# Loads, casts and weight issues of the first two chunks put in a new order, in a windowed-attention and max-out FFN kernel

## The chip, the cores and the metric

The kernel runs on one core of a Trainium2 chip. The metric is the device time of one execution in microseconds (us), lower is better; a kernel's time is the median of its runs.

The core's engines each work through a list of instructions of their own, in the order in which the program names them: TensorE (PE, with its weight loads shown apart as PEld), VectorE (DVE), ScalarE (ACT), GpSimd (POOL) and SyncE (SP). An engine waits on semaphores where an instruction needs another engine's result, and whatever stands behind the waiting instruction on that engine waits too. Transfers from HBM run on 16 DMA engines; here SP issues the loads of Q, K and V and the stores, and POOL issues the loads of the weights, which turn float32 into bf16 on the way.

## The reference

Attention with a window of 128 positions and 4 sink positions, for 4 batches, 8 heads, 768 positions and 64 columns; then a feed-forward layer whose hidden value is the maximum of three products.

```python
scores = scale * np.matmul(q, k.transpose(0, 1, 3, 2))      # 4 x 8 x 768 x 768
keep = is_sink | in_window                                  # pos < 4, or 0 <= i - j < 128
scores = np.where(keep, scores, -1000000000.0)
a = np.exp(scores - np.max(scores, axis=-1, keepdims=True))
a = a / (np.sum(a, axis=-1, keepdims=True) + 1e-09)
attn_out = np.matmul(a, v)
x = attn_out.transpose(0, 2, 1, 3).reshape(3072, 512)
h = np.maximum(np.maximum(x @ w1, x @ w2), x @ w3)          # 512 x 768 each
return (h @ w_out).astype(np.float32)                       # 768 x 512
```

## The kernel before

The 3072 rows are cut into 12 chunks of 256, three to a batch. A chunk holds 128 partitions of two neighbouring rows each. For every chunk the kernel

- loads Q, K and V (`load`, L107), 512 KB each, as float32; with `parts=2` a load is cut into two halves of four heads, `part=0` for heads 0 to 3 and `part=1` for heads 4 to 7. A `gate` writes one element of the target on POOL first, so that the load can't be issued before POOL has come to that place;
- casts Q and K to bf16, in halves of four heads (`cast_qk`, L118), and V in four pieces of 64 partitions (`cast_v`, L123), straight into `vb`, which has a column of ones beside each head;
- transposes Q and K by PE through PSUM (`turn`, L138, copied out at L142 for Q and L149 for K; `turn2`, L164, does the same for a half of K and then of Q in one PSUM bank, copied out at L171 and L168);
- computes scores for a pair of heads (`score`, L331), for which `premask` may first write the mask into PSUM by a matmul with the identity (L311); exponentials on ACT (`expo`, L398); where there was no premask, a multiplication by the mask on DVE (`mask`, L406);
- scores the sink positions (`sink_score`, L423, its exponential at L427) and takes their V rows out by a matmul with a selector (`sink_v`, L437), which DVE copies into `vs` (L440). In the second and third chunk of a batch the output sum begins with them: `av_open` multiplies them (L453) into four PSUM banks, one for each pair of heads, and reads `vs`;
- multiplies by V (`av`, L471) and divides by the sum (`norm`, L481 and L484, on DVE; `then=False` leaves it to a later call);
- transposes the result (`xpose`, L496, copied out at L498) and runs the FFN: `ffn_h(ci, fp, wi)` (L524) multiplies chunk ci by a third `fp` of weight `wi`, 8 matmuls of 256 columns. For `wi = 0` the product is copied out (L536), for the other two the maximum is taken (L540). `ffn_y` (L553) makes the output.

The weights come in nine thirds of 256 columns (`load_w`, L292). `warm(n)` (L203) gives PE n matmuls on zeros whose result nobody reads.

The order of all of it is written out by hand, from L639 on; every call appends its instructions to its engines' lists there and then. PSUM has eight banks, handed out in the order in which they were given back; a bank's next user waits for the last reader of it. The change and the prediction's steps touch the part from L639 to L718, up to the loads of weight 2. In it chunk 0 has no rows before it and no sink scores, so its `av_open` does no matmuls; chunk 1 is the first with L453. The calls behind L718, from `expo(1, 2)` on, stand in both kernels in the same order.

In the kernel before, chunk 0 is worked through pair by pair of heads (2, 3, 0, 1), the load of V of chunk 1 is issued with those of Q and K, and its two casts on DVE stand ahead of the copies of chunk 0's transposed result.

Of the kernel before, what the change touches and what calls it, by code (L numbers as in the profile page):

```python
# [16 lines left out]
def kernel(  # L17
# [31 lines left out]
    with tc.manual_schedule():  # L49
# [43 lines left out]
        def load(ci, what="kqv", gate=None, part=None, parts=1, eng=None):  # L93
            if ci >= NCH:
                return
            b, c = divmod(ci, CPB)
            t0 = c * 256
            for w in what:
                src = {"k": k, "q": q, "v": v}[w]
                if (ci, w) not in raws:  # L100
                    raws[ci, w] = raw.tile([128, H, 2, D], F32, tag=w + "_raw", name=w + "_raw")
                dst = raws[ci, w]
                if gate is not None:
                    gate(dst[0:1, 0, 0, 0:1])
                n = H // parts
                for g in range(parts) if part is None else (part,):
                    (eng or nc.sync).dma_start(  # L107
                        out=dst[:, n * g:n * g + n],
                        in_=src[b, n * g:n * g + n, t0:t0 + 256]
                            .rearrange("h (p i) d -> p h (i d)", i=2))  # L110
# [7 lines left out]
            f(x[:, 2 * g:2 * g + 2].rearrange("q p i a d -> q p a i d"),  # L118
              y[:, 4 * g:4 * g + 4].rearrange("q (p a) i d -> q p a i d", a=2))

        def cast_v(ci, n, i, eng):
            if ci < NEW:
                eng.tensor_copy(  # L123
                    vb[ci % RING][64 * i:64 * i + 64, n, :, 0:D],
                    raws[ci, "v"][64 * n:64 * n + 64, :, i])
                return
            for h in range(2):
                x, y = 64 * h + 32 * i, 64 * n + 32 * h
                eng.tensor_copy(  # L129
                    vb[ci % RING][x:x + 32, n, :, 0:D], raws[ci, "v"][y:y + 32, :, i])  # L130
# [67 lines left out]
        def warm(n):  # L198

            if n:  # L200
                pw = bank([128, 512], F32, "warm")
                for _ in range(n):
                    nc.tensor.matmul(pw, lhsT=wz[:, 0:128], rhs=wz, start=True, stop=True)  # L203
                give(pw)
# [187 lines left out]
        def expo(ci, p):  # L392
            if ci >= NEW:
                return expo4(ci, p)
            lo = 0 if ci % CPB else 1
            e, st = es[ci, p]
            for a in range(2):
                nc.scalar.activation(e[:, a, lo:], st[a][:, lo:], AF.Exp, scale=scale)  # L398
                give(st[a])
# [237 lines left out]


        load(0, 'q', part=1, parts=2)  # L639
        warm(8)  # L640
        load(0, 'k')
        load(0, 'q', part=0, parts=2)
        load(0, 'v', part=0, parts=2, gate=pool_gate)
        cast_qk(0, 'q', 1, nc.scalar)
        load(0, 'v', part=1, parts=2)
        masks()
        sink_init()
        factors(msk, addm)
        turn(0, 'q', 1, nc.scalar)
        warm(4)  # L650
        premask(0, (2,))
        cast_qk(0, 'k', 0, nc.scalar)
        cast_qk(0, 'k', 1, nc.vector)
        turn(0, 'k', 1, nc.vector)
        load(1, 'k')
        turn(0, 'k', 0, nc.scalar)
        cast_qk(0, 'q', 0, nc.gpsimd)
        premask(0, (3,))
        score(0, (2,))
        score(0, (3,))  # L660
        turn(0, 'q', 0, nc.vector)
        premask(0, (0,))
        load(1, 'q')
        expo(0, 2)
        cast_v(0, 1, 0, nc.gpsimd)
        cast_v(0, 0, 0, nc.vector)
        cast_v(0, 1, 1, nc.vector)
        cast_v(0, 0, 1, nc.vector)
        load_w(0, 512, 768)
        load(1, 'v')  # L670
        score(0, (0,))
        expo(0, 3)
        cast_qk(1, 'k', 0, nc.gpsimd)
        premask(0, (1,))
        score(0, (1,))
        expo(0, 0)
        expo(0, 1)
        load_w(0, 256, 512)
        av_open(0)
        av(0, 2)  # L680
        av(0, 3)
        turn2(1, 'k', 0, nc.vector)
        cast_qk(1, 'k', 1, nc.scalar)
        av(0, 0)
        cast_qk(1, 'q', 0, nc.gpsimd)
        cast_qk(1, 'q', 1, nc.scalar)
        turn(1, 'k', 1, nc.scalar)
        load_w(0, 0, 256)
        av(0, 1)
        premask(1, (0,))  # L690
        turn2(1, 'q', 0, nc.vector)
        sink_k(0)
        premask(1, (1,))
        turn(1, 'q', 1, nc.scalar)
        cast_v(1, 0, 0, nc.vector)
        cast_v(1, 1, 0, nc.vector)
        load_w(1, 512, 768)
        xpose(0, 0, nc.vector)
        score(1, (0,))
        score(1, (1,))  # L700
        expo(1, 0)
        expo(1, 1)
        load_w(1, 256, 512)
        cast_v(1, 1, 1, nc.gpsimd)
        xpose(0, 1, nc.vector)
        cast_v(1, 0, 1, nc.gpsimd)
        load_w(1, 0, 256)
        score(1, (3,))
        sink_score(1)
        load(2, 'k', part=0, parts=2, gate=after(0, 300))  # L710
        load(2, 'k', part=1, parts=2)
        sink_v(0)
        expo(1, 3)
        ffn_h(0, 2, 0, 1, nc.vector)
        score(1, (2,))
        load(2, 'q', part=1, parts=2)
        load(2, 'q', part=0, parts=2, gate=pool_gate)
        load_w(2, 0, 256)  # L718
# [281 lines left out]
```

## Time and profile before

| | us |
|---|---|
| median of 3 runs | 175.81 |
| lowest and highest | 175.04, 176.0 |
| span of the profiled execution | 173.5 |
| PE busy | 167.7 |
| DVE, ACT, POOL busy | 125.1, 88.8, 110.1 |

The profiled execution's own time is its span, from the first to the last instruction; the page gives no other. The granted clock of TensorE was full in all of its 40 slices. The page's first part gives the busy time of each engine and its share of the span, its second part the same in 40 slices of 4.3 us, in tenths. The chain of work is followed back from the last instruction: at each step to whatever released it. Matmuls overlap, so that a busy PE isn't yet PE at its peak. Idle time of an engine that isn't the bottleneck costs nothing by itself. In the rows of a timeline the first number is the start in us from the start of the span, the second the time covered by the x instructions of the row.

### The profile page before, as it was taken

What the parts mean: (1) busy time and instruction counts of PE and PEld (TensorE: products, weight loads), DVE (VectorE), ACT (ScalarE), POOL (GpSimd) and SP (SyncE); (2) the same over time, 40 slices, a digit from 0 to 9 for tenths busy, and PEclk for the clock granted to TensorE, in tenths of its full rate; (3) what the DMA queues carried; (4) which work ended last, traced back from release to release, by engine and by line L of the source; (5) the groups of instructions that cost most, each with busy time, mean ns of one, the idle gap of its engine ahead of it and who ended that gap; (6) DMA issues with size and microseconds to landing.
All of it is one profiled execution on the core that took longest, in us unless ns stands there. A gap on an engine that the chain in (4) does not pass through costs nothing.

```text
span 173.5 us, 5418 instructions
## 1 busy us (share of the span) xinstructions
PE 167.7 (97%) x2225; PEld 129.2 (74%) x2225; DVE 125.1 (72%) x262; ACT 88.8 (51%) x183; POOL 110.1 (63%) x193
## 2 busy tenths in 40 slices
PE   7979999999999999999999999999999999999992
PEld 2546889857695697797797797797897896896871
DVE  3187856696697985986877977877778876776361
ACT  4598554587944615817726717627636516510210
POOL 7389507445399999999999999999998700000000
PEclk9999999999999999999999999999999999999999
DMA  4999999999996999988999969969999119017303
GB/s 134 300 289 198 216 217 252 219 274 290 292 210 118 250 264 180 252 188 220 264 186 247 264 165 254 257 163 238 257 176 274 32 34 376 21 35 272 121 2 121
DMA packets 71545, 35.22 MB, mean 203 GB/s; under 512 B 27488, under 2 KB 69984, under 8 KB 71520
## 3 DMA queue, kind: packets, MB, share of 16 engines
q1 hardware_dynamic: 65824, 31.60, 79.0%
q0 software_dynamic: 5552, 3.15, 12.8%
q8 instruction: 17, 0.28, 0.7%
q10 hardware_dynamic: 144, 0.13, 0.2%
q14 instruction: 8, 0.07, 0.1%
HBM read 25.17 MB, written 6.29 MB: 181 GB/s over the span
## 4 chain that ended last, share of the span: by engine, by line
PE 93%; DVE 3%; ACT 1%; issue 0%
PE h_ps L524 55%; PE y_ps L577 11%; PE y_ps L553 7%; PE o L471 7%; PE st L357 3%; PE warm L203 3%; PE st L331 3%; PE pt L138 2%; ACT e_sb L398 1%; PE o L453 1%; DVE x_sb L484 1%; PE sk L423 1%; PE y_ps L599 1%; DVE vb L123 1%; PE xt L496 1%; PE st L311 0%
## 5 line engine op out<-in xcount | busy, mean ns | idle before, releaser
L524 PE MATMUL h_ps<-xT,w 128*128 128x256 bf16 x864 | 101.2, 273 | 0.1
L524 PEld LDWEIGHTS <-w 128*128 128x128 bf16 x864 | 81.9, 98 | 9.9 <-issue 0.3
L540 DVE TENSOR_TENSOR h_sb<-h_sb,h_ps 128x512 bf16<-128x512 bf16 (+1 forms) x74 | 49.3, 671 | 20.0 <-PE h_ps L524 16.0
L536 ACT CAST h_sb<-h_ps 128x512 bf16<-128x512 f32 x35 | 20.5, 585 | 52.2 <-PE h_ps L524 52.2
L129 POOL CAST vb<-v_raw 32x512 bf16<-32x512 f32 x48 | 36.7, 764 | 2.8 <-DMA v_raw<-in_v_dram 0.6
L90 POOL CAST k_bf<-k_raw 32x512 bf16<-32x512 f32 x48 | 29.5, 614 | 2.2
L398 ACT ACTIVATE e_sb<-st 128x512 bf16<-128x512 f32 (+1 forms) x48 | 23.1, 588 | 0.7 <-PE st L331 0.7
L484 DVE TENSOR_TENSOR x_sb<-o,rc 128x256 bf16<-128x256 f32 x48 | 20.4, 424 | 1.6
L577 PE MATMUL y_ps<-wo,h_sb 64*64 64x512 bf16 (+1 forms) x312 | 21.1, 377 | 0.0
L471 PE MATMUL o<-vb,e_sb 128*128 128x65 bf16 x352 | 16.8, 193 | 0.4 <-ACT e_sb L398 0.4
L471 PEld LDWEIGHTS <-e_sb 128*128 128x128 bf16 x352 | 14.6, 97 | 2.8 <-issue 0.8
L123 POOL CAST vb<-v_raw 64x512 bf16<-64x512 f32 x18 | 12.4, 691 | 5.8 <-DMA v_raw<-in_v_dram 5.2
L389 DVE TENSOR_TENSOR e_sb<-e_part,msk 128x1024 bf16<-128x1024 bf16 x16 | 13.5, 865 | 3.1 <-ACT e_part L374 3.0
L406 DVE TENSOR_TENSOR e_sb<-e_sb,msk 128x1024 bf16<-128x1024 bf16 (+1 forms) x18 | 13.3, 756 | 2.1 <-ACT e_sb L398 2.0
L577 PEld LDWEIGHTS <-h_sb 64*64 64x64 bf16 (+1 forms) x312 | 9.9, 106 | 5.0
L374 ACT ACTIVATE e_part<-st 128x384 bf16<-128x384 f32 x32 | 13.1, 496 | 0.5 <-PE st L357 0.5
L553 PE MATMUL y_ps<-wo,h_sb 128*128 128x512 bf16 x54 | 13.0, 380 | 0.0
L481 DVE RECIPROCAL rc<-o 128x4 f32<-128x4 f32 x48 | 8.3, 174 | 3.5 <-PE o L471 3.4
L118 POOL CAST k_bf<-k_raw 128x512 bf16<-128x512 f32 x6 | 3.8, 647 | 9.6 <-DMA k_raw<-in_k_dram 9.4
L553 PEld LDWEIGHTS <-h_sb 128*128 128x128 bf16 x54 | 4.8, 97 | 5.6 <-DVE h_sb L540 0.9
L118 ACT CAST q_bf<-q_raw 128x512 bf16<-128x512 f32 x13 | 7.6, 621 | 2.0 <-DMA q_raw<-in_q_dram 1.9
L427 ACT ACTIVATE e_sink<-sk 128x256 bf16<-128x256 f32 x8 | 3.1, 389 | 10.0 <-PE sk L423 10.0
(90 smaller groups left out, 144.2 us busy)
## 6 DMA issues: line engine op xcount, KB each, us to landing
k_raw<-in_k_dram SPq DMA_DIRECT2D x11, 512.0 KB, 5.7
v_raw<-in_v_dram SPq DMA_DIRECT2D x11, 512.0 KB, 5.8
q_raw<-in_q_dram SPq DMA_DIRECT2D x10, 512.0 KB, 6.5
out_dram<-y_sb SPq DMA_DIRECT2D x9, 512.0 KB, 3.1
w<-in_moe_w_dram POOLq DMA_DIRECT2D x9, 256.0 KB, 6.6
q_raw<-in_q_dram SPq DMA_DIRECT2D x4, 256.0 KB, 7.7
out_dram<-y_sb SPq DMA_DIRECT2D x1, 1024.0 KB, 5.2
wo<-in_moe_w_out_dram POOLq DMA_DIRECT2D x2, 384.0 KB, 7.4
```

The lines of the kernel that those rows point to most:

```text
L90: f(bfs[ci, "k"][x:x + 32, :, n], raws[ci, "k"][y:y + 32, :, i].rearrange("q (p a) d -> q p a d", a=2))
L123: eng.tensor_copy(vb[ci % RING][64 * i:64 * i + 64, n, :, 0:D], raws[ci, "v"][64 * n:64 * n + 64, :, i])
L129: eng.tensor_copy(vb[ci % RING][x:x + 32, n, :, 0:D], raws[ci, "v"][y:y + 32, :, i])
L389: nc.vector.tensor_mul(x.rearrange("q a (t s) c -> q (a t) s c", t=2), y, msk2)
L398: nc.scalar.activation(e[:, a, lo:], st[a][:, lo:], AF.Exp, scale=scale)
L471: nc.tensor.matmul(o[:, t, a], lhsT=e[:, a, s], rhs=vb[cv % RING][:, n, 2 * p + a], start=first, stop=True, skip_group_check=True)
L484: nc.vector.tensor_mul(xs[ci][:, p], o[:, :, :, 0:D], rc.unsqueeze(3).to_broadcast([128, 2, 2, D]))
L524: nc.tensor.matmul(hp[:, f].rearrange("q (i t r) -> q i t r", i=2, r=x.shape[3]), lhsT=w_sb[wi][:, ds, c0:c0 + 128], rhs=x, start=(ds == 0 ...
L536: (nc.scalar.copy if eng is nc.scalar else eng.tensor_copy)(dst, hp)
L540: nc.vector.tensor_max(dst[:, x], dst[:, x], hp[:, x])
L553: nc.tensor.matmul(yp, lhsT=hs[ci][:, fb, t * 128:(t + 1) * 128], rhs=wo[:, fb], start=(fb == 0), stop=(fb == FB - 1))
L577: nc.tensor.matmul(yps[ci][t][c:c + cols], lhsT=hs[ci][hp, fb, x:x + cols], rhs=wo[hp, fb], start=(turn == 0 and fb == 0), stop=(turn == 1 ...
```

## The change

Loads: K of chunk 0 comes in two halves, heads 4 to 7 first, and V's halves also in that order and without a gate; K and Q of chunk 1 are issued right behind. V of chunk 1 gets a gate on POOL, behind POOL's issue of the first third of weight 0.

Casts and copies of chunk 0: the first Q half is cast by DVE and not ACT, K's second half by ACT and not DVE; the copies of its transposes are DVE's. `cast_v` can take half of the heads, and V of chunk 0 is cast in eight pieces, four on POOL and four on DVE, heads 4 to 7 first. The exponentials follow their scores at once.

Chunk 1: its K halves are cast by POOL (heads 4 to 7) and ACT in place of the reverse, and `turn(1, 'k', 1)` stands ahead of `turn2(1, 'k', 0)`; `norm(0, 0)` follows these. The copies of its Q go to ACT (heads 0 to 3) and DVE. `premask(1, (1,))` and `score(1, (1,))` stand behind the second `xpose` of chunk 0; `ffn_h(0, 2, 0)` stands ahead of `score(1, (3,))`, and the casts of V of chunk 1 stand behind that `ffn_h`. `sink_v(0)` and `score(1, (2,))` stand ahead of the loads of chunk 2.

Filling matmuls: `warm(8)` and `warm(4)` become `warm(7)`, `warm(1)` and `warm(2)`, the last two among the `av` calls of chunk 0.

```diff
-        def cast_v(ci, n, i, eng):
+        def cast_v(ci, n, i, eng, g=None):
             if ci < NEW:
+                hh = slice(0, H) if g is None else slice(4 * g, 4 * g + 4)
                 eng.tensor_copy(
-                    vb[ci % RING][64 * i:64 * i + 64, n, :, 0:D],
-                    raws[ci, "v"][64 * n:64 * n + 64, :, i])
+                    vb[ci % RING][64 * i:64 * i + 64, n, hh, 0:D],
+                    raws[ci, "v"][64 * n:64 * n + 64, hh, i])
                 return
...
         load(0, 'q', part=1, parts=2)
-        warm(8)
-        load(0, 'k')
+        warm(7)
+        load(0, 'k', part=1, parts=2)
+        load(0, 'k', part=0, parts=2)
         load(0, 'q', part=0, parts=2)
-        load(0, 'v', part=0, parts=2, gate=pool_gate)
-        cast_qk(0, 'q', 1, nc.scalar)
         load(0, 'v', part=1, parts=2)
+        load(0, 'v', part=0, parts=2)
+        load(1, 'k')
+        load(1, 'q')
         masks()
         sink_init()
         factors(msk, addm)
-        turn(0, 'q', 1, nc.scalar)
-        warm(4)
+        cast_qk(0, 'q', 1, nc.vector)
+        cast_qk(0, 'k', 1, nc.scalar)
+        turn(0, 'q', 1, nc.vector)
         premask(0, (2,))
+        turn(0, 'k', 1, nc.vector)
         cast_qk(0, 'k', 0, nc.scalar)
-        cast_qk(0, 'k', 1, nc.vector)
-        turn(0, 'k', 1, nc.vector)
-        load(1, 'k')
-        turn(0, 'k', 0, nc.scalar)
-        cast_qk(0, 'q', 0, nc.gpsimd)
         premask(0, (3,))
         score(0, (2,))
+        expo(0, 2)
         score(0, (3,))
+        expo(0, 3)
+        cast_qk(0, 'q', 0, nc.gpsimd)
+        turn(0, 'k', 0, nc.vector)
         turn(0, 'q', 0, nc.vector)
         premask(0, (0,))
-        load(1, 'q')
-        expo(0, 2)
-        cast_v(0, 1, 0, nc.gpsimd)
-        cast_v(0, 0, 0, nc.vector)
-        cast_v(0, 1, 1, nc.vector)
-        cast_v(0, 0, 1, nc.vector)
-        load_w(0, 512, 768)
-        load(1, 'v')
+        cast_v(0, 0, 0, nc.gpsimd, 1)
+        cast_v(0, 1, 0, nc.gpsimd, 1)
+        cast_v(0, 0, 1, nc.vector, 1)
+        cast_v(0, 1, 1, nc.vector, 1)
         score(0, (0,))
-        expo(0, 3)
-        cast_qk(1, 'k', 0, nc.gpsimd)
         premask(0, (1,))
         score(0, (1,))
         expo(0, 0)
         expo(0, 1)
-        load_w(0, 256, 512)
+        cast_v(0, 0, 0, nc.gpsimd, 0)
+        cast_v(0, 1, 0, nc.gpsimd, 0)
+        cast_v(0, 0, 1, nc.vector, 0)
+        cast_v(0, 1, 1, nc.vector, 0)
+        load_w(0, 512, 768)
+        load(1, 'v', gate=pool_gate)
         av_open(0)
         av(0, 2)
+        warm(1)
         av(0, 3)
+        cast_qk(1, 'k', 1, nc.gpsimd)
+        cast_qk(1, 'k', 0, nc.scalar)
+        load_w(0, 256, 512)
+        av(0, 0, then=False)
+        turn(1, 'k', 1, nc.scalar)
         turn2(1, 'k', 0, nc.vector)
-        cast_qk(1, 'k', 1, nc.scalar)
-        av(0, 0)
+        norm(0, 0)
+        av(0, 1)
+        warm(2)
         cast_qk(1, 'q', 0, nc.gpsimd)
         cast_qk(1, 'q', 1, nc.scalar)
-        turn(1, 'k', 1, nc.scalar)
         load_w(0, 0, 256)
-        av(0, 1)
         premask(1, (0,))
-        turn2(1, 'q', 0, nc.vector)
+        turn2(1, 'q', 0, nc.scalar)
+        turn(1, 'q', 1, nc.vector)
         sink_k(0)
+        load_w(1, 512, 768)
+        xpose(0, 0, nc.vector, (2, 3, 0, 1))
+        score(1, (0,))
+        expo(1, 0)
+        xpose(0, 1, nc.vector, (2, 3, 0, 1))
         premask(1, (1,))
-        turn(1, 'q', 1, nc.scalar)
+        score(1, (1,))
+        expo(1, 1)
+        load_w(1, 256, 512)
+        ffn_h(0, 2, 0, 1, nc.vector)
+        cast_v(1, 1, 1, nc.gpsimd)
         cast_v(1, 0, 0, nc.vector)
         cast_v(1, 1, 0, nc.vector)
-        load_w(1, 512, 768)
-        xpose(0, 0, nc.vector)
-        score(1, (0,))
-        score(1, (1,))
-        expo(1, 0)
-        expo(1, 1)
-        load_w(1, 256, 512)
-        cast_v(1, 1, 1, nc.gpsimd)
-        xpose(0, 1, nc.vector)
         cast_v(1, 0, 1, nc.gpsimd)
         load_w(1, 0, 256)
         score(1, (3,))
         sink_score(1)
+        expo(1, 3)
+        sink_v(0)
+        score(1, (2,))
         load(2, 'k', part=0, parts=2, gate=after(0, 300))
         load(2, 'k', part=1, parts=2)
-        sink_v(0)
-        expo(1, 3)
-        ffn_h(0, 2, 0, 1, nc.vector)
-        score(1, (2,))
         load(2, 'q', part=1, parts=2)
```

## The prediction

> **What bounds the kernel now.** I read the page first, then the table of busy time in stretches, then the chain of work that ended last over the first 26 us, and last the timeline of the same stretch. Of the page:
>
> ```profile
> span 173.5 us, 5418 instructions
> ...
> PE 167.7 (97%) x2225; PEld 129.2 (74%) x2225; DVE 125.1 (72%) x262; ACT 88.8 (51%) x183; POOL 110.1 (63%) x193
> ...
> PE   7979999999999999999999999999999999999992
> ```
>
> TensorE bounds it, and the only slices with a hole lie at the start. The table (columns: stretch, length, busy PE, PEld, DVE, ACT, POOL, granted clock, DMA share, GB/s) says where the holes end:
>
> ```profile
> 9.00:12.00 3.00, 2.12 (x34) 1.33 (x34) 2.38 (x8) 2.85 (x8) 2.57 (x4) 1.00 1.17 290
> 12.00:15.90 3.90, 3.67 (x61) 2.46 (x61) 3.66 (x12) 3.12 (x7) 3.72 (x7) 1.00 1.37 221
> 17.20:22.00 4.80, 4.80 (x77) 4.24 (x76) 4.12 (x12) 2.81 (x7) 2.68 (x7) 1.00 1.41 217
> 22.00:30.00 8.00, 8.00 (x79) 7.20 (x78) 4.45 (x8) 3.96 (x7) 2.99 (x5) 1.00 1.28 229
> 30.00:169.00 139.00, 139.00 (x1919) 108.90 (x1917) 106.19 (x211) 69.77 (x146) 91.82 (x150) 1.00 0.89 200
> ```
>
> From 17.2 us on PE never stands idle: 151.8 busy of 151.8. The program of both kernels is the same from there on. So one moment decides: the start of av_open(1), the sink matmuls of chunk 1 on L453. Work ahead of it is paid only if it delays that start; a start that comes x later ends the kernel x later.
>
> ```profile
> 15.88 1.03 PE h_ps L524 x8
> 16.92 0.33 PE st L331 x6
> 17.24 0.34 PE o L453 x8
> ```
>
> In the chain of work, piece by piece (start, length), the first FFN matmuls (h_ps, 15.88) lead to a score and then straight to L453 at 17.2.
>
> **The change, part by part.** The change touches the stretch before 17.2 only, so I follow it along the engines' orders, with durations from these rows (start, length, then the instruction; a bracket is idle time and what ended it):
>
> ```profile
> 6.71 0.61 POOL L118 CAST q_bf<-q_raw 128x512 bf16<-128x512 f32 x1 [1.46 <-DMA q_raw<-in_q_dram]
> ...
> 7.33 0.42 DVE L149 COPY kT<-pt 128x512 bf16<-128x512 bf16 x1 [1.13 <-PE pt L138]
> ...
> 9.16 0.34 PE L331 MATMUL st<-qT,kT 64*128 64x256 bf16 x4 [0.19 <-DVE qT L142]
> ...
> 10.39 0.60 POOL L118 CAST k_bf<-k_raw 128x512 bf16<-128x512 f32 x1
> ...
> 12.09 0.62 ACT L118 CAST q_bf<-q_raw 128x512 bf16<-128x512 f32 x1 [0.24 <-DMA q_raw<-in_q_dram]
> ...
> 12.12 0.61 POOL L118 CAST q_bf<-q_raw 128x512 bf16<-128x512 f32 x1 [0.43 <-DMA q_raw<-in_q_dram]
> ...
> 12.32 0.59 PE L311 MATMUL st<-addm,ident 128*128 128x512 bf16 x2
> ...
> 12.79 0.40 PE L164 MATMUL pt<-ident,q_bf 128*128 128x128 bf16 x4
> ...
> 13.82 1.56 POOL L292 DMA_DIRECT2D w<-in_moe_w_dram  x2
> ...
> 13.88 0.58 ACT L142 COPY qT<-pt 128x512 bf16<-128x512 bf16 x1 [0.69 <-PE pt L138]
> 13.90 1.18 DVE L123 CAST vb<-v_raw 64x512 bf16<-64x512 f32 x2
> ...
> 14.90 0.40 PE L331 MATMUL st<-qT,kT 64*128 64x128 bf16 x6
> ...
> 15.89 0.29 DVE L440 CAST vs<-sv 128x130 bf16<-128x130 f32 x1 [0.16 <-PE sv L437]
> ...
> 16.36 0.42 ACT L427 ACTIVATE e_sink<-sk 128x256 bf16<-128x256 f32 x1
> ...
> 16.62 2.12 ACT L398 ACTIVATE e_sb<-st 128x512 bf16<-128x512 f32 x4
> ...
> 16.95 0.69 DVE L536 CAST h_sb<-h_ps 128x512 bf16<-128x512 f32 x1 [0.77 <-PE h_ps L524]
> ...
> 17.18 0.41 PE L453 MATMUL o<-vs,e_sink 32*128 32x130 bf16 x8
> ```
>
> *Loads of chunk 0 in halves, Q and K of chunk 1 issued without a gate.* The DMAs already run full (290 GB/s in the row 9 to 12), and the bytes ahead of K and Q of chunk 1 are the same. So these land as before: the casts behind them start at 10.39 and 12.09. Only the first K half comes earlier. Below this I set no gain; above, none is excluded but what SP waited, which is rival 3.
>
> *Casts shared out anew.* Heads 0 to 3 of Q are cast by POOL at 6.71 to 7.32; transposes 0.40, then DVE copies K's half (0.42) and Q's (0.42): score(0,(0,)) at about 8.4, not 9.16. A gain of 0.7 in the first stage.
>
> *V in quarters.* Eight casts in the place of four, each of half the columns, four of them on DVE; two DVE casts of the old size took 1.18, so four halves take about 1.2 and end near 9.6, those of heads 4 to 7 near 9.0. av(0,2) and av(0,3) can go at 9.2. But the next item on PE's list is turn(1,k,1), and its cast on POOL cannot start before the landing shown by 10.39: cast to 11.0, transposes at 11.1, turn2(1,k,0) to 11.7, its DVE copy to 12.15. PE stands idle for about 1.1 us before them. norm(0,0) and norm(0,1) stand behind that copy and end near 13.25. The first stage's lead is spent here at no cost, as the next load sets the pace anyway.
>
> *Chunk 1's Q.* Landed at 12.1: POOL cast to 12.73, transposes 12.79 to 13.19, ACT copy (0.58, 13.23 to 13.81): score(1,(0,)) at 13.87. Then in PE's new order xpose(0,1) (four transposes, some 0.24 before the next starts, 0.1 of turn-round on either side), premask(1,1) (0.59 for two, of which 0.43 before the next starts), score(1,1) (0.40, of which 0.2) put ffn_h(0,2,0) at about 15.2, against 15.88. Ends: 15.0 with no turn-rounds, 15.6 if weight 0's third comes late (rival 1). DVE's xT copies end at 14.9 and are covered.
>
> *The order on DVE behind it.* This is where I see the loss. Before, DVE had the two casts of chunk 1's V at 13.90, ahead of everything, and copied vs (sink_v) at 15.89, well before 17.18. Now its order is: evacuation of ffn_h(0,2,0), cast_v(1,0,0), cast_v(1,1,0), then the copy of vs; and av_open(1) reads vs. So from the start of ffn_h: 1.07 until the evacuation starts (15.88 to 16.95), 0.69 for it, two casts, 0.29 for vs, 0.06 until PE goes (as from 12.73 to 12.79). For the casts the same two took 1.18 beside two POOL issues (13.82, 1.56); now one issue, that of w1's last third, lies beside them. Lower end 0.84 (the five such casts of this kernel were 0.42 at the shortest):
>
> ```profile
> L123 DVE CAST vb<-v_raw x5: 422/481/745, 9.0 to 14.3; 64x512 bf16<-64x512 f32 x5
> ```
>
> Upper end: the whole POOL issue, half of 1.56, waited out on top, 1.6. I take 1.0, nearer to the 1.18 that is the same work. [...]
>
> Sum: 15.2 + 1.07 + 0.69 + 1.0 + 0.29 + 0.06 = 18.3, against 17.18: later by 1.1. Meanwhile PE has only score(1,3), sink_score, sink_v and score(1,2) to do, under 1 us; the rest is idle.
>
> *A second chain to the same place.* av_open's fourth bank is that of score(1,3)'s second half, so expo(1,3) must have read it. sink_score now follows ffn_h: 15.2 + 0.9 + 0.2 for score(1,3) + 0.35 until its exponential (0.42), then expo(1,3), 0.26 later (16.36 to 16.62), 0.48 to its second half and 0.67 for that (2.12 for four): 18.1. So taking the casts out of DVE's way would win back only 0.2.
>
> *V of chunk 1 behind the first third of weight 0.* The issues before, their times to landing, and the packets of each queue (q1 the loads, q0 the weights; count, MB) in 9.2 to 12.7 and, last two, in 22 to 28:
>
> ```profile
> 6.52 1.71 SPq L107 DMA_DIRECT2D v_raw<-in_v_dram  x1
> ...
> 9.17 1.11 POOL L292 DMA_DIRECT2D w<-in_moe_w_dram  x1
> ```
> ```profile
> v_raw<-in_v_dram SPq DMA_DIRECT2D x1, 512.0 KB, 7.4
> ```
> ```profile
> w<-in_moe_w_dram POOLq DMA_DIRECT2D x1, 256.0 KB, 5.7
> ```
> ```profile
> q1 hardware_dynamic: 2014, 1.01, 116.4%
> ```
> ```profile
> q0 software_dynamic: 1282, 0.64, 77.2%
> q1 hardware_dynamic: 1269, 0.63, 52.0%
> ```
>
> Before, V landed at 13.9 and the third at 14.9. The third, issued at 9.17, moved no packet up to 12.7; I take it that the loads ahead held it. Now POOL issues it at about the same time and V's gate follows near 10.4. V's place ahead of it is gone, and V took 13.9 - 12.1 = 1.8: third near 13.2, V some 2 us behind it, near 15.2. V's casts on DVE are due at 16.95, those on POOL, in its order, from 15.4: both covered. Past 16.95, each us of V costs one. The gate's memset is 0.1 on POOL. On SP nothing stands behind V until chunk 2's loads, whose gate waits for weights as before.
>
> *Moved issues.* Weight thirds leave POOL up to 0.3 later (w1's last at 16.75 for 16.61); the queue has five ahead by then, and PE asks for its weights 1.1 later: nothing. Warm matmuls, twelve to ten, at most 0.43 each, all lie in waits for landings: nothing.
>
> ```profile
> 1.26 3.60 PE L203 MATMUL warm<-wz 128*128 128x512 bf16 x8 [1.26 <-DVE wz L192]
> ...
> 5.08 1.67 PE L203 MATMUL warm<-wz 128*128 128x512 bf16 x4
> ...
> 6.91 0.61 PE L138 MATMUL pt<-ident,k_bf 128*128 128x128 bf16 x8
> ```
>
> The warm ones go at half pace (0.43 each), the transposes at 6.91 at full. If the full pace came later, up to 9 or so, the first stage would slip by some 0.4, still inside the wait for chunk 1's K: nothing; above that, its lead of 0.7 is the reserve.
>
> Total: span 173.5 + 1.1 = 174.6. The median of the runs shown is 175.81, 2.3 above the profiled span; I carry that over: 176.9. A measurement of this kernel tells a difference from none at about 0.5%, 0.9 us.
>
> **The rivals.** 1: *weight 0's third or V comes late.* Either the software queue needs more than 2 us from the end of its issue (10.3) to its first packet, whatever lies ahead; then V overtakes the third, both share, and the third lands near 15.5: ffn_h at 15.6, total +1.5. Or both are ready at 11.5 and share as in 22 to 28, at 0.63 MB in 6 us, 0.105 a us: V's 0.52 MB takes 5 us and lands near 17; its casts then run beside POOL's: total +1.3 to +1.6. For the first: the empty queue up to 12.7. Against: it would have become ready just as the loads ended. For the second: the two equal counts. I take 177.3 for both. [...]
>
> 2: *The late start is absorbed.* Busy is not peak: were there slack in the 151.8 us, a start 1.1 later would end where it did: 175.8. Against it, the weight loads of the matmuls, one after another on their unit, fill 7.20 of 8.00 in 22 to 30, and not one stretch shows PE idle.
>
> 3: *The lead lasts, not slower.* Q of chunk 1 lands earlier, since SP no longer waits (SP's own queue, who it waited for, total, times, longest):
>
> ```profile
> SPq L107 <- POOL sel L270: 0.7, 1, 0.7
> ```
>
> Each us of an earlier landing moves ffn_h and av_open(1) by one. It decides from 1.1, a landing at 11.0: then 175.8. Against: the loads run at 290 GB/s without a pause, and 0.7, all that SP waited, would give 176.2.
>
> **How the numbers follow.** Forecast, +0.5 to +1.6 by the bounds of the cast term and of the start of ffn_h: 0.62. Rival 1, +1.3 to +2.0: 0.2. Rival 2, 0 to +0.4: 0.11. Rival 3, below +0.4: 0.07. The forecast's own range is 176.3 to 177.4. The range of eight in ten leaves out rival 3, part of rival 2 and the extreme of rival 1: 175.9 to 177.8. Slower by over 0.5% (above 176.7): two thirds of the forecast and rival 1 whole, 0.61; within 0.5%: the rest of the forecast, rival 2 and part of rival 3, 0.34; faster: the rest of rival 3, 0.05.
>
> **What would show it.** In the profile after: score(0,(0,)) near 8.4; casts behind K and Q of chunk 1 still near 10.4 and 12.1; the first h_ps near 15.2; on DVE the order L536, L123 twice, L440, ending near 18.2; the first L453 near 18.3 with a wait on DVE (or on ACT's expo) before it, and no wait on PE after it. Wrong if L453 starts before 17.5, if Q of chunk 1 is cast before 11.5, or if L453 is late but the span is not.

## The result and the profile after

The changed kernel takes 177.24 us (median of six runs) and the kernel before 175.79 (six runs too): a ratio of 1.0093, with a 95% interval of 1.0071 to 1.0114. That is 1.45 us more by the medians and 1.6 by the ratio; the forecast was 176.9, slower by 1.1, with a range of its own from 176.3 to 177.4. The size was right. Where it comes from was only partly right, and this is what the rest is about. Medians here and below are of all runs and ratios of the undisturbed ones alone: one of the changed kernel's six runs took 217.89 us at a mean granted clock of 0.758 and is left out of its ratio.

The page of the changed kernel, the lines that answer to those of the kernel before:

```profile
span 175.2 us, 5410 instructions
...
PE 166.7 (95%) x2217; PEld 128.9 (74%) x2223; DVE 126.8 (72%) x265; ACT 87.9 (50%) x181; POOL 111.2 (63%) x196
...
PE   7879799999999999999999999999999999999991
```

PE is busy for 1 us less in a span that is 1.7 longer. The timeline from 12 us on shows the place that the forecast spoke of (start, length, instruction; in brackets idle time and what ended it):

```profile
12.42 0.61 POOL L118 CAST q_bf<-q_raw 128x512 bf16<-128x512 f32 x1
...
14.97 0.42 DVE L499 COPY xT<-xt 128x512 bf16<-128x512 bf16 x1 [0.40 <-PE xt L497]
...
15.63 1.05 PE L525 MATMUL h_ps<-xT,w 128*128 128x256 bf16 x8
16.45 1.27 POOL L124 CAST vb<-v_raw 64x512 bf16<-64x512 f32 x2 [0.84 <-DMA v_raw<-in_v_dram]
...
16.71 0.69 DVE L537 CAST h_sb<-h_ps 128x512 bf16<-128x512 f32 x1 [1.31 <-PE h_ps L525]
...
17.32 1.32 DVE L124 CAST vb<-v_raw 64x512 bf16<-64x512 f32 x2
...
18.56 0.27 DVE L441 CAST vs<-sv 128x130 bf16<-128x130 f32 x1
...
18.88 0.29 PE L454 MATMUL o<-vs,e_sink 32*128 32x130 bf16 x8 [1.27 <-DVE vs L441]
...
19.11 0.66 PE L472 MATMUL o<-vb,e_sb 128*128 128x65 bf16 x16
```

(Lines from L124 on are numbered one higher than before.) The sink matmul starts at 18.88, where it started at 17.18, and what it waits for is the copy of vs, behind the evacuation and the two V casts on DVE. This is the step that the forecast named, 0.6 larger.

The end tells something else. The last pieces of the chain of work, first of the kernel before, then of the changed one:

```profile
169.92 0.23 PE y_ps L599 x2
170.15 0.02 issue
170.18 0.42 DVE y_sb L601
```
```profile
170.15 1.32 PE y_ps L600 x12
171.47 0.02 issue
171.49 0.42 DVE y_sb L602
```

PE ends at 170.15 and 171.47, 1.32 later; the span is 1.74 longer. Of the 1.70 at the sink matmul 0.38 has been absorbed on the way, and 0.42 has been added after PE's last instruction. These 0.42 are not PE's, nor the stores': the last store lands 2.4 us after PE's end in both. They lie in the program's closing waits. SP's own queue in the last 10 us (line, who it waited for, total, times, longest), before and after:

```profile
SPq L995 <- DMA out_dram<-y_sb: 1.7, 3, 0.8
```
```profile
SPq L1003 <- DMA out_dram<-y_sb: 2.1, 1, 2.1
```

At the end SP goes through nine waits for transfers, one after another. Before, the last three of them are real ones, and only the ninth ends after the last landing. After, the second waits out the whole 2.1 us, and seven more that are met by then still have to be gone through. In the trace these follow one another by 0.061 us: 7 x 0.061 = 0.43. From the last landing to the end of the span it is 0.92 before and 1.35 after. The changed kernel issues one transfer more on SP (K of chunk 0 in two pieces), and the last store's wait stands elsewhere in the order.

### The profile page after: what moved, and what is told of

The parts are those of the page before. It is cut to its first block, busy times and chain, and to the rows that moved or that the text cites. A ratio compares the mean times of both kernels' runs of the same rounds, so it can differ in the third digit from the quotient of the medians.

```text
span 175.2 us, 5410 instructions
## 1 busy us (share of the span) xinstructions
PE 166.7 (95%) x2217; PEld 128.9 (74%) x2223; DVE 126.8 (72%) x265; ACT 87.9 (50%) x181; POOL 111.2 (63%) x196
## 4 chain that ended last, share of the span: by engine, by line
PE 89%; DMA 3%; POOL 2%; DVE 1%; SPq 1%; issue 1%; ACT 0%; POOLq 0%
PE h_ps L525 54%; PE y_ps L578 11%; PE y_ps L554 7%; PE o L472 6%; PE st L358 3%; DMA v_raw<-in_v_dram 3%; PE st L332 3%; PE pt L139 1%; SPq L107 1%; PE o L454 1%; POOL vb L124 1%; PE y_ps L600 1%; DVE vb L124 1%; PE xt L497 1%; PE sk L424 1%
## 5 line engine op out<-in xcount | busy, mean ns | idle before, releaser
L124 POOL CAST vb<-v_raw 64x512 bf16<-64x512 f32 (+1 forms) x21 | 12.9, 616 | 5.7 <-DMA v_raw<-in_v_dram 5.0
L407 DVE TENSOR_TENSOR e_sb<-e_sb,msk 128x1024 bf16<-128x1024 bf16 (+1 forms) x18 | 13.2, 753 | 1.9 <-ACT e_sb L399 1.8
L332 PE MATMUL st<-qT,kT 64*128 64x128 bf16 (+1 forms) x128 | 7.5, 238 | 0.5 <-DVE kT L150 0.2
```

What stands on the lines that cost most here:

```text
L124: eng.tensor_copy(vb[ci % RING][64 * i:64 * i + 64, n, hh, 0:D], raws[ci, "v"][64 * n:64 * n + 64, hh, i])
L407: (eng or nc.vector).tensor_mul(e[:, :, lo:], e[:, :, lo:], msk0[0] if lo else msk)
```

## The experiments

The kernels of one group ran on one chip, beside runs of the kernel before (median 175.67 in the first group, 175.43 in the second, 175.45 in the third). Ratios are to those runs, with a 95% interval; they are not exactly the quotient of the two medians.

| kernel | median | ratio | interval |
|---|---|---|---|
| front_old_back_new | 176.20 | 1.0020 | 0.9994 to 1.0046 |
| front_new_back_old | 176.54 | 1.0051 | 1.0025 to 1.0077 |
| after_v_ungated | 176.95 | 1.0087 | 1.0059 to 1.0115 |
| after_k_whole | 177.56 | 1.0103 | 1.0062 to 1.0144 |
| before_k_halves | 177.11 | 1.0081 | 1.0048 to 1.0113 |
| before_v_quarters | 175.66 | 1.0018 | 0.9986 to 1.0051 |
| before_v_casts_late | 175.46 | 1.0029 | 0.9995 to 1.0064 |
| after_sink_v_first | 176.99 | 1.0062 | 1.0030 to 1.0095 |
| after_sinks_first | 177.15 | 1.0081 | 1.0054 to 1.0109 |
| before_k_halves_low_first | 177.23 | 1.0079 | 1.0046 to 1.0113 |
| before_casts_behind_vs | 175.62 | 0.9984 | 0.9952 to 1.0015 |

**The two halves of the change.** The change has a front (all up to `turn2(1, 'q', 0)`: loads, casts and scores of chunk 0, K of chunk 1) and a back (from there: the order around `ffn_h`, the V casts and `sink_v`). The first kernel has the old front and the new back, the second the new front and the old back; V of chunk 1 has no gate in either. The core of the back, as the first has it:

```diff
-        turn2(1, 'q', 0, nc.vector)
+        turn2(1, 'q', 0, nc.scalar)
+        turn(1, 'q', 1, nc.vector)
...
+        ffn_h(0, 2, 0, 1, nc.vector)
+        cast_v(1, 1, 1, nc.gpsimd)
         cast_v(1, 0, 0, nc.vector)
         cast_v(1, 1, 0, nc.vector)
...
+        expo(1, 3)
+        sink_v(0)
+        score(1, (2,))
...
-        sink_v(0)
-        expo(1, 3)
-        ffn_h(0, 2, 0, 1, nc.vector)
-        score(1, (2,))
```

> The first part as before (up to av(0,1): whole K, whole V casts, V of chunk 1 issued with the loads), the second part (from premask(1,(0,)) to the loads of chunk 2) as changed. Theory (the loss is the order on DVE behind ffn_h): Q of chunk 1 is cast at 12.1 as before, ffn_h starts near 15.3, its copy-out ends near 17.1, two casts and the copy of vs put the first sink matmul (L454) near 18.4; end about 1.2 us above the kernel before, 177.0 in all. Rival (the loss is the later landings of the first part): sink matmul near 17.3, end within 0.2 us of before.

> The first part as changed, but V of chunk 1 issued right behind Q and without a gate; the second part as before. Theory: the lead of the first stage is lost in the wait for K and Q of chunk 1; Q is cast at 12.1 to 12.4, DVE's casts of V and the copies of xT behind it set the first ffn_h at 15.9 to 16.2 and the sink matmul at 17.2 to 17.5: within 0.3 us of before. Rival (the new first part gains, the new second part hides it): 0.5 us or more below before.

The new back alone gives 176.20, 0.53 above the kernel before, with an interval that still holds no change. In its trace all that was foreseen on DVE is there:

```profile
17.44 0.96 DVE L124 CAST vb<-v_raw 64x512 bf16<-64x512 f32 x2
...
18.31 0.28 DVE L441 CAST vs<-sv 128x130 bf16<-128x130 f32 x1
...
18.65 0.29 PE L454 MATMUL o<-vs,e_sink 32*128 32x130 bf16 x8 [0.91 <-DVE vs L441]
```

The sink matmul starts 1.5 later than in the profiled execution of before, but the median is only 0.5 higher. The new front alone gives 176.54, 0.87 above, though nothing in it had been given a price. So by the medians the loss has two sources, and the forecast had one, the back; clear of no change is only the other, the front.

**The gate of V.** In after_v_ungated V of chunk 1 is issued right behind Q and K of chunk 1:

```diff
+        load(1, 'v')
         masks()
...
-        load(1, 'v', gate=pool_gate)
```

> The changed kernel with V of chunk 1 issued right behind Q of chunk 1 and without a gate; all else as changed. Theory: V lands near 14.2 in place of 16.4, the DMA rate has no hole between 11 and 13 us, but DVE reaches V's casts only behind the copy-out, so the sink matmul comes at 18.6 to 18.8 against 18.9: 0.1 to 0.3 us below the changed kernel. Rival (late V is the cause): the sink matmul falls by 1 us or more, to below 17.9.

176.95, a ratio 0.06% below the changed kernel's own: the gate is worth nothing that can be measured. Without it V lands at 14.1 and the sink matmul starts at 18.48. With it the DMAs have a hole between the loads and the weights (table by stretch of the changed kernel; the last number is GB/s):

```profile
11.00:12.00 1.00, 0.36 (x7) 0.36 (x8) 0.58 (x3) 0.43 (x1) 1.00 (x2) 1.00 0.99 157
12.00:13.00 1.00, 0.95 (x14) 0.58 (x12) 0.66 (x3) 0.92 (x2) 0.85 (x3) 1.00 0.69 67
```

V was issued at 10.94, the third of weight 0 at 9.87, and still the queues ran nearly empty; why isn't shown. Of these bytes only V was waited for, by POOL, which stood idle 0.84 before its two casts of it (the row at 16.45 above).

**K of chunk 0 whole, in the changed kernel** (after_k_whole):

```diff
-        load(0, 'k', part=1, parts=2)
-        load(0, 'k', part=0, parts=2)
+        load(0, 'k')
```

> The changed kernel with K of chunk 0 loaded whole in one DMA, all else as changed. If the two halves of K make the hole in the DMA rate between 4.0 and 5.25 us (192 GB/s in the changed kernel, 330 before), the rate stays above 300 there, Q of chunk 1 is cast near 12.1 in place of 12.4, and the sink matmul comes 0.2 to 0.4 us earlier, near 18.6. If the hole has another cause (the number of DMAs queued by then), it stays and nothing moves by more than 0.1.

177.56: no gain. In its trace PE, with five filling matmuls fewer at the start and no early half of K to work on, stands idle from 5.1 to 6.6 us, and after that goes back to half pace for 3.4 us (the granted clock is the third number from the right):

```profile
5.00:6.00 1.00, 0.07 (x1) 0.00 (x0) 0.20 (x1) 0.04 (x1) 0.44 (x1) 1.00 1.17 295
...
7.00:8.00 1.00, 0.80 (x9) 0.38 (x8) 0.42 (x1) 0.09 (x1) 0.71 (x2) 0.74 1.18 291
8.00:9.00 1.00, 1.00 (x13) 0.71 (x8) 0.06 (x1) 0.92 (x3) 0.88 (x3) 0.50 1.15 289
9.00:10.00 1.00, 1.00 (x8) 0.38 (x7) 0.97 (x3) 0.72 (x2) 0.94 (x3) 0.50 1.18 292
10.00:11.00 1.00, 1.00 (x6) 0.17 (x6) 0.91 (x4) 0.56 (x2) 0.93 (x3) 0.56 1.12 282
```

The first FFN matmuls start at 16.6. The half pace is not all of it: two of its four runs had a mean granted clock of 0.988, and the two without were no faster. Its closing waits are the short ones of the kernel before, so all of its loss lies ahead of PE's end, at 172.05 (171.47 in the changed kernel). The new front is built for K in halves and is no better without; whether the cut itself costs, this kernel can't say.

**The cut alone, and V's quarters alone, in the kernel before.** First before_k_halves, then before_v_quarters; beside them a second look at the unchanged kernel, to see how far two traces of one program lie apart.

```diff
-        load(0, 'k')
+        load(0, 'k', part=1, parts=2)
+        load(0, 'k', part=0, parts=2)
```
```diff
-        load(0, 'v', part=0, parts=2, gate=pool_gate)
+        load(0, 'v', part=1, parts=2, gate=pool_gate)
...
-        load(0, 'v', part=1, parts=2)
+        load(0, 'v', part=0, parts=2)
...
-        cast_v(0, 1, 0, nc.gpsimd)
-        cast_v(0, 0, 0, nc.vector)
-        cast_v(0, 1, 1, nc.vector)
-        cast_v(0, 0, 1, nc.vector)
+        cast_v(0, 0, 0, nc.gpsimd, 1)
+        cast_v(0, 1, 0, nc.gpsimd, 1)
+        cast_v(0, 0, 1, nc.vector, 1)
+        cast_v(0, 1, 1, nc.vector, 1)
+        cast_v(0, 0, 0, nc.gpsimd, 0)
+        cast_v(0, 1, 0, nc.gpsimd, 0)
+        cast_v(0, 0, 1, nc.vector, 0)
+        cast_v(0, 1, 1, nc.vector, 0)
```

> The kernel before with K of chunk 0 loaded in two halves, heads 4 to 7 first; nothing else. If two halves thin the DMA stream between 4 and 5.5 us (as in the three traces that have them), the rate there falls below 260 GB/s, Q of chunk 1 is cast 0.2 to 0.5 us later and the end moves with it: 0.2 to 0.5 us slower. If not, within 0.15 us of before.

> The kernel before with V of chunk 0 cast in eight pieces, four on POOL and four on DVE, heads 4 to 7 first, and its loads in that order; nothing else. The quarter takes POOL 0.40, so POOL spends 1.6 in place of 0.61, and its next items (first weight third, K cast of chunk 1, second third) leave about 1.0 later: turn2(1,k,0) waits for the K cast. Theory (the quarters cost POOL's time and chunk 1's K): 0.3 to 0.7 us slower. Rival (chunk 1's Q sets the pace): within 0.2 us of before.

> The kernel before once more, for a second trace of it. If the landings of chunk 0's and chunk 1's loads are fixed by the program, K of chunk 1 is cast near 10.4 and Q near 12.1 again. If they scatter from run to run, as the four other traces suggest (Q of chunk 1 cast at 12.1 to 12.65), they lie up to 0.5 us later here too, and the first sink matmul with them, near 17.5.

V in quarters costs nothing measurable, as forecast. The cut of K, by itself, costs about as much as the whole change: 177.11, which is 1.7 more by the medians and 1.4 by the ratio. And the second look (175.62) shows K landing at 6.15 where it was 5.76, Q of chunk 1 at 12.47 where it was 12.07, and the sink matmul at 17.55 where it was 17.18. So landings differ by 0.4 us between executions of one program, and a difference of that size between two single traces says nothing.

**The cut again, the other half first.** If it mattered which heads come first, this kernel should be as fast as before.

```diff
-        load(0, 'k')
+        load(0, 'k', part=0, parts=2)
+        load(0, 'k', part=1, parts=2)
```

> The kernel before with K of chunk 0 in two halves, heads 0 to 3 first (ACT's half), where the earlier experiment had heads 4 to 7 first. Same number of transfers, other order. If the cut itself costs (one more issue of 0.55 on SP, a thinner stream near 4 to 5.5 us, landings that scatter more), the time is again 0.6 to 0.9% above the kernel before, 176.6 to 177.2, and Q of chunk 1 is cast at 12.3 to 12.7. If the loss of the earlier one came of which half came first, or of the moment at which PE reached its full pace in those executions, the time is within 0.3% of the kernel before, 175.3 to 176.0.

177.23: the same loss. It is the cut, not which half comes first. Three things can be read from the traces.

First, the closing waits. SP's row at the end reads "1.7, 3, 0.8" in all seven kernels whose K comes whole, and "2.1, 1, 2.1" in all seven with K cut, the changed kernel among them; from the last landing to the end it is 0.90 to 0.92 in the former and 1.33 to 1.35 in the latter. That is 0.43 of the 1.4 to 1.7 us. In after_k_whole, which has all of the change but the cut, the old sequence is back. No run added a transfer at another place, so that it is the count that does it is the reading of the two sequences, not a test.

Second, the stream of the loads, which looks like a cause and isn't shown to be one. In the stretch 4 to 5.5 us the seven with K whole moved 311 to 334 GB/s, the seven with K cut 211 to 283. The rows of that stretch and of 14 to 20 us, of the kernel before, of before_k_halves and of before_k_halves_low_first:

```profile
4.00:5.50 1.50, 1.50 (x8) 0.57 (x6) 0.00 (x0) 0.79 (x2) 1.19 (x2) 1.00 1.14 325
14.00:20.00 6.00, 5.77 (x98) 4.52 (x97) 4.78 (x12) 5.32 (x11) 5.84 (x11) 1.00 1.45 196
```
```profile
4.00:5.50 1.50, 1.50 (x8) 0.68 (x6) 0.83 (x1) 0.62 (x2) 1.20 (x2) 1.00 0.95 269
14.00:20.00 6.00, 5.57 (x99) 4.17 (x97) 5.00 (x12) 5.13 (x11) 5.91 (x11) 1.00 1.33 173
```
```profile
4.00:5.50 1.50, 1.50 (x8) 0.55 (x6) 0.00 (x0) 0.76 (x2) 1.21 (x2) 1.00 1.01 283
14.00:20.00 6.00, 5.73 (x94) 4.12 (x93) 4.57 (x12) 4.85 (x10) 4.89 (x11) 1.00 1.28 154
```

But the stretch is too short to judge by. Before it, from 0 to 4 us, the two with K cut moved more (141 and 127 GB/s for 118), and from 0 to 9 us the three moved 225, 219 and 220 GB/s: as many bytes as before. The changed kernel, at 214, lacks 0.05 MB by then, or 0.2 us at the 290 GB/s that follow. Q of chunk 1 landed at 12.07 to 12.53 in the seven with K whole and at 12.07 to 12.81 in the others, 0.2 later on the mean, which is less than the 0.4 by which two traces of one program differ.

Third, in these two traces the weights also came more slowly, 173 and 154 GB/s from 14 to 20 us for 196, and in the second of them it shows on PE at chunk 2:

```profile
28.98 0.61 POOL L118 CAST k_bf<-k_raw 128x512 bf16<-128x512 f32 x1 [7.29 <-DMA k_raw<-in_k_dram]
...
29.65 0.40 PE L138 MATMUL pt<-ident,k_bf 128*128 128x128 bf16 x4 [0.41 <-POOL k_bf L118]
```

There its PE ends at 171.83 (170.15 before): 0.6 of it at the sink matmul, the rest in stalls behind it. But front_new_back_old and after_v_ungated, with K cut too, show 187 and 193 GB/s in that stretch, and front_old_back_new, with K whole, 178. So the slow weights aren't shown to come of the cut, and of its 1.4 to 1.7 us only the 0.43 is accounted for; the rest stays open.

**DVE's order, in the kernel before.** Two kernels move the two V casts behind the copies of xT: before_v_casts_late puts them right behind the second `xpose` and so ahead of `sink_v(0)`, as shown, and before_casts_behind_vs right behind `sink_v(0)`.

```diff
-        cast_v(1, 0, 0, nc.vector)
-        cast_v(1, 1, 0, nc.vector)
         load_w(1, 512, 768)
...
         xpose(0, 1, nc.vector)
+        cast_v(1, 0, 0, nc.vector)
+        cast_v(1, 1, 0, nc.vector)
         cast_v(1, 0, 1, nc.gpsimd)
```

> The kernel before with DVE's two casts of V of chunk 1 moved behind both copies of xT and ahead of the copy of vs; nothing else. Theory (these casts delay the copies of xT, and these the first ffn_h): the copies of xT end near 14.8 in place of 15.7, ffn_h starts near 15.3, the sink matmul near 16.85, then held by the sink's exponential: 0.2 to 0.35 us faster than before. Rival (the order of the casts matters only where they lie behind the copy-out of ffn_h): within 0.1 us.

> The kernel before with cast_v(1,0,0) and cast_v(1,1,0) moved behind sink_v(0), so that neither the copies of xT nor that of vs stand behind them on DVE. If DVE's order ahead of the sink matmul has something to give, xT is copied by 15.4, ffn_h starts near 15.9, vs is copied by 16.3, the casts run 16.3 to 17.5 ahead of the evacuation, and the sink matmul starts 0.2 to 0.3 earlier than in the kernel before: 175.2. If the casts now make the evacuation or av(1,0) late, 175.6 to 176.0.

Neither gains. In the first, vs waits behind the casts and the sink matmul behind vs (0.29). In the second everything comes earlier but the end:

```profile
15.74 0.29 DVE L440 CAST vs<-sv 128x130 bf16<-128x130 f32 x1 [0.23 <-PE sv L437]
15.95 1.17 DVE L123 CAST vb<-v_raw 64x512 bf16<-64x512 f32 x2
...
16.94 0.23 PE L453 MATMUL o<-vs,e_sink 32*128 32x130 bf16 x3
...
17.39 0.27 PE L453 MATMUL o<-vs,e_sink 32*128 32x130 bf16 x5 [0.22 <-ACT e_sb L398]
...
17.59 0.66 PE L471 MATMUL o<-vb,e_sb 128*128 128x65 bf16 x16
```

The sink matmuls start 0.24 earlier than in the kernel before, stop after three of them for expo(1,3), and `av` starts at 17.59, where it was 17.52. It is the second chain that the forecast had named, a bank that expo(1,3) reads: its exponential of the first half of score(1,3) ends at 17.34, and the fourth matmul starts at 17.39.

**DVE's order, in the changed kernel.** The first kernel moves `sink_v(0)` alone ahead of `ffn_h(0, 2, 0)`, the second all that leads to the sink matmul.

```diff
+        sink_v(0)
         ffn_h(0, 2, 0, 1, nc.vector)
...
         expo(1, 3)
-        sink_v(0)
         score(1, (2,))
```
```diff
+        score(1, (3,))
+        sink_score(1)
+        expo(1, 3)
+        sink_v(0)
         ffn_h(0, 2, 0, 1, nc.vector)
...
-        score(1, (3,))
-        sink_score(1)
-        expo(1, 3)
-        sink_v(0)
         score(1, (2,))
```

> The changed kernel with sink_v(0) put ahead of ffn_h(0,2,0), so that DVE copies vs before the evacuation and the two V casts; nothing else moved. Theory (the prediction's second chain): vs is ready by 16.3, but the sink matmul then waits for the bank that expo(1,3) reads, whose second half ended about 18.5 in the changed kernel's trace; so it starts near 18.5 instead of 18.88, and the time falls by 0.3 to about 176.9. Rival (DVE's order is the whole of it): the sink matmul starts once e_sink is ready, near 17.8, 1.1 earlier, and the time falls to about 176.1. Rival (what counts lies ahead of Q's landing): no measurable change, 177.2.

> The changed kernel with score(1,3), sink_score(1), expo(1,3) and sink_v(0) all ahead of ffn_h(0,2,0), as they stand in the kernel before. Both chains to the sink matmul are then short: ffn_h near 16.3, sink matmul near 17.5 where the changed kernel has 18.88. If the order behind Q's landing costs what the medians of the exchange of the two halves gave (0.5), the time is about 176.7, and what is left over the kernel before is the front's 0.9. If it costs what single traces showed (1.0 to 1.3), the time is about 176.0.

The first:

```profile
15.58 0.29 DVE L441 CAST vs<-sv 128x130 bf16<-128x130 f32 x1 [0.53 <-PE sv L438]
...
17.16 1.26 DVE L124 CAST vb<-v_raw 64x512 bf16<-64x512 f32 x2
...
17.55 0.29 PE L454 MATMUL o<-vs,e_sink 32*128 32x130 bf16 x8 [0.16 <-ACT e_sink L428]
...
17.77 0.36 PE L472 MATMUL o<-vb,e_sb 128*128 128x65 bf16 x5
...
18.46 0.49 PE L472 MATMUL o<-vb,e_sb 128*128 128x65 bf16 x11 [0.33 <-DVE vb L124]
```

The sink matmuls start 1.33 earlier than in the changed kernel, at once when e_sink is there, and all eight go through. But the casts of V, still behind the evacuation, now hold up `av` in the middle. PE's last matmul ends at 170.85 (171.47 in the changed kernel), and the time is 176.99. In the second kernel the sink matmul starts at 17.74, and both waits come in turn, for expo(1,3) (here for its second half, which ends at 18.37) and then for V:

```profile
17.74 0.40 PE L454 MATMUL o<-vs,e_sink 32*128 32x130 bf16 x3
...
18.42 0.27 PE L454 MATMUL o<-vs,e_sink 32*128 32x130 bf16 x5 [0.28 <-ACT e_sb L399]
...
19.12 0.49 PE L472 MATMUL o<-vb,e_sb 128*128 128x65 bf16 x11 [0.18 <-DVE vb L124]
```

177.15. By their ratios, 0.3% and 0.1% below the changed kernel's, DVE's order is worth 0.2 to 0.6 us, in line with the exchange of the backs (0.53), and not the 1.3 to 1.7 by which single sink matmuls move. The interval of the exchange holds no change, and the other two overlap with the changed kernel's, so none of the three is clear of no effect. No kernel was faster than the one before by more than could be told from no change.

## Why the prediction was right, and where it was not

*One moment decides: the start of L453.* This step held only in part. In the changed kernel 1.32 of the 1.70 arrived at PE's end. But from that start to the end of PE's work it is 152.97 us before (170.15 less 17.18), 152.59 after, 153.30 with `sink_v` first, 154.05 in the cut with the low heads first. An earlier start was given back in large part at the next waits, for a bank of expo(1,3) and for V's casts, and a later one partly absorbed, by 0.38 in the changed kernel. That is a part of what rival 2 said. In front_new_back_old's trace it went the other way: the sink matmul starts 0.42 later than before and PE ends 1.05 later, so most of that loss arose behind the moment that was to decide. And a fixed sum behind PE's end was taken for granted, where 0.43 was added.

*The order on DVE.* The mechanism was right: evacuation, casts, vs, then the sink matmul, with the wait on DVE before it, as foretold. The terms: ffn_h at 15.63 (15.2; Q of chunk 1 was cast at 12.42, 0.3 later than in the trace of before), evacuation 1.08 later (1.07) and 0.69 long (0.69), casts 1.32 (1.0) and vs done at 18.83. From there to the sink matmul 0.05 (0.06). The casts lie inside the range given.

Taken singly, the first took 0.69 (17.32 to 18.01), beside a cast on POOL that ended at 17.72, and the second 0.62 (18.02 to 18.64), beside an issue on POOL that ended at 18.41; the shortest such cast of the kernel before took 0.42. A DVE cast of this size that ran beside one on POOL ended 0.28 to 0.29 behind it, in the changed kernel (18.01 and 17.72), in the kernel before (9.51 and 9.22) and in before_casts_behind_vs (17.12 and 16.84). In these traces POOL's issues held a cast up for a part of their length at most: the second cast here was 0.20 longer where the issue ran on for 0.39, and in front_old_back_new a cast and an issue start together at 17.97 and take 0.42 and 0.74, no longer than others. So the term was 0.3 larger mostly for a cast on POOL that the forecast had placed earlier, not for an issue waited out whole.

As a price for the time, 1.1 was about twice too large: the medians give 0.2 to 0.6, and even these aren't clear of nothing.

*The second chain: taking the casts out of DVE's way wins back only 0.2.* This step failed in its working. The program hands PSUM's banks out in the order in which they were given back; followed through it, the fourth bank of `av_open(1)` is that of the first half of score(1,3), in the kernel before and in the changed one, and not of the second. Of the 18.1 that I had worked out, the second half's part was too much, some 0.5. And the order decides which bank it is: with `sink_v` first the fourth bank is that of sink_score, and expo(1,3) has no part in the wait, so the sink matmul started 1.33 earlier (Q landed 0.3 earlier there as well). With all sinks first, the third and fourth banks are those of both halves of score(1,3), and the second half binds. In the time, `sink_v` first won only 0.3%, for another reason: V's casts become the wait.

*The lead of the first stage is spent at no cost; loads in halves land as before.* This is the step that failed most. The new front costs 0.87 by itself, and the cut of K alone 1.4 to 1.7 in the old front; so the new front seems to win back about half of what the cut loses, though in the new front K whole gained nothing. I had priced the cut by bytes alone ("the bytes ahead are the same"). The landings don't contradict that: Q of chunk 1 landed at 12.37, where the kernels with K whole have 12.07 to 12.53. What went wrong is that the landings were taken for all that the cut could touch: 0.43 came in at the other end of the kernel, which no row that I read had to do with. Where the rest of the front's cost arises stays open.

*First stage.* score(0,(0,)) came at 8.80, not 8.4:

```profile
7.23 0.61 POOL L118 CAST q_bf<-q_raw 128x512 bf16<-128x512 f32 x1 [1.95 <-DMA q_raw<-in_q_dram]
...
8.80 0.34 PE L332 MATMUL st<-qT,kT 64*128 64x256 bf16 x4 [0.19 <-DVE qT L143]
```

Heads 0 to 3 of Q landed later, at 7.17, where the kernels with K whole have 6.66 to 7.15, so that POOL cast them at 7.23 and not at 6.71. PE then stood idle 0.92 before turn(1,k,1) (1.1 foretold), at 11.64 and not 11.1, K of chunk 1 having landed 0.5 later. As foretold, this lead bought nothing.

*V and weight 0's third.* The third landed at 14.69 (13.2 foretold) and V at 16.40 (15.2), as the queues ran nearly empty in between. V's casts on DVE were due at 17.32, so they were still covered, by 0.9. Those on POOL were not: POOL waited 0.84 for V, and its casts came to lie beside DVE's. In after_v_ungated they don't, DVE's two casts take 0.96 and the sink matmul starts 0.4 earlier; the median says that this is worth nothing measurable. Rival 1 did not come about: ffn_h wasn't late for want of weights. The first of its two ways is closed as well: the third's first packet came at 11.53, 0.7 after the end of its issue, so here the software queue did not need 2 us by itself; in the kernel before it came at 12.85, 2.6 after, behind the loads ahead, as I had taken it. Rival 3 neither: Q came no earlier.

*V in quarters, and the filling matmuls, at nothing.* Right in both places that test it: 175.66 with quarters, and in the changed kernel PE reached its full pace at 6.2, well before chunk 1. DVE's four casts of V of chunk 0 took 1.61 in the changed kernel, where 1.2 was reckoned, still inside the wait for K of chunk 1. In after_k_whole, though, the hole on PE where four filling matmuls had stood (0.07 busy of the us from 5 on) was followed by a loss of the pace (a granted clock of 0.50 from 8 to 10).

*The sum.* 1.45 us in the medians: 0.43 from the closing waits, 0.53 from the new back, 0.44 from the rest of the front (0.87 less 0.43), 0.05 unassigned, each of the last three uncertain by about 0.5. The forecast's 1.1, all of it from the back, came out near this by luck: a term about twice too large stood in for two that were missing.

## What to carry to other kernels

Cutting one transfer in two was not free though the bytes were the same: in the kernel before it cost 0.8%, a part of it at the far end of the kernel, so compare the closing waits of two traces before you look for the difference in the work. A single instruction's start is a poor measure of what an order is worth; look for the next two waits behind it, and for differences below 0.5 us trust medians and not single traces, as two traces of one program lay 0.4 apart in their landings. Judge a stream of loads by the bytes moved up to a moment, not by the rate in a short stretch. If you move a copy that many wait for ahead of casts that nobody waits for yet, count the casts as the next wait, and look anew which bank each later instruction gets.

## What was unexpected in the hardware

*When PE gets its full pace.* The first matmul starts at 1.26 in the trace of the kernel before and at 1.27 in that of the changed one, and the moment at which matmuls go from half to full pace lies between 4.1 and 7.3 us. Both are estimates from the lengths of rows: four transposes from 4.35 on took 0.40 in after_k_whole; in before_k_halves four from 4.65 on still took 0.63, and eight from 7.35 on took 0.61. The four filling matmuls of the kernel before in its second look, and the same four in before_k_halves (start, length):

```profile
4.86 1.03 PE L203 MATMUL warm<-wz 128*128 128x512 bf16 x4
```
```profile
5.08 1.91 PE L203 MATMUL warm<-wz 128*128 128x512 bf16 x4
```

The first four run 0.22 apart, the second 0.43. What sets the moment isn't shown; from first to last it is 3.2 us. The granted clock shows 1.00 in these stretches, and in the first slices of the profile's page too, so the pace has to be read from the matmuls. In after_k_whole it fell back for 3.4 us (a granted clock of 0.74, 0.50, 0.50 and 0.56 in the us from 7, 8, 9 and 10 on), behind a stretch in which PE had been busy for 0.96, 0.07 and 0.37 of the us from 4, 5 and 6 on.

*Small casts on POOL.* A quarter of V takes POOL 0.40, a piece twice its size 0.61 to 0.63: by an estimate from these two, close to half of the small cast's time doesn't go with its size.

*The stream of the loads and the number of transfers.* The thinner stream at 4 to 5.5 us with K cut, in seven traces of seven (211 to 283 GB/s, where K whole has 311 to 334), was not foreseen. Why it thins isn't shown: all loads of chunk 0 had been issued by 4.1 us. In the kernel before with K cut it is made up for by 9 us (219 and 220 GB/s from 0 to 9 us, for 225).
